# A fused attention and two-MLP block on one core: the mask stored once, block means in half the products, and a re-ordered front

## The chip, the cores and the metric

The kernel runs on one core of one Trainium2 chip. The metric is the device time of one execution in microseconds (us), the median of several runs; lower is better. The engines are PE (TensorE: matrix products, with its weight loads shown apart as PEld), DVE (VectorE), ACT (ScalarE), POOL (GpSimd) and SP (SyncE, which here issues all DMA transfers). Each engine works through its own list of instructions in order, and waits on semaphores for the others.

## The reference, cut to what matters

Two batches of 768 tokens, 8 heads of 64. An attention over near keys and block maxima feeds a token mixer, and that feeds a gated channel MLP.

```python
k_sum = k.reshape(B, H, 24, 32, D).max(axis=3)        # block maxima
v_sum = v.reshape(B, H, 24, 32, D).mean(axis=3)       # block means
scores_l = where(|i - j| < 16, scale * q @ k.T, -1e9) # near keys: the mask
scores_s = scale * q @ k_sum.T + log(32)              # far: 24 block maxima
a = softmax(concatenate([scores_l, scores_s]))
x = a @ concatenate([v, v_sum])                       # (2, 768, 512) after the heads are joined
h = relu(x.T @ w_tok1) @ w_tok2                       # token mixer
u = x + h.T
x2 = u + relu(u @ w_ch1) @ w_ch2                      # channel mixer
# then: token shift, k = relu(xk @ w_k), v = k*k @ w_v, r = sigmoid(xr @ w_r)
out = r * v
```

## The kernel before

The attention is worked in 12 *units* of 128 queries, 6 for each batch (units 0 to 5 and 6 to 11). For a unit, PE writes scores of 8 heads against the 64 near keys of each 32-query block and against the 24 block maxima (`sc`), and adds the mask by two more products (L304): the mask is split into an indicator of the query's place in its block (128 columns) and rows of 0 or -1e30 over 64 keys, four times side by side for the four head pairs, in three kinds (first unit, middle, last). Both stand in the 34 upper partitions of each half of the tile `msk`, so `load_mask` issues two loads of 34 partitions x 896 numbers. DVE takes maxima and subtracts them (`max`, L309 and L311), ACT takes the exponentials (`en`, `ef`), PE transposes them (`tr`, L337), ACT copies them out (`tc`, L341), and PE multiplies them with the values and the block means (`pv`, L348 and L355). DVE divides (`norm`), ACT and DVE split the result into a high and a low part (`xh`, `xl`), and PE multiplies these with the token weights (`t1`, three products of 128x512 at L191 to L193 for each half). After six units the hidden rows are split by `t1h` (ACT, L464) and `t1l` (DVE), and `t2` multiplies them with the second token weights on top of transposes of x (L497 and L505).

The block means come from `vs`: 13 steps a batch, each with 4 products of a 128x64 indicator with 65 columns of one head group of the values (L272). `vd` copies them to where `pv` reads them. `vu` (POOL) fills the overlapping value windows.

The weights arrive as pairs of 64-bit words and are turned into F32 by `ca` (ACT, L395), an optional `cn` (ACT, L402), and `cj` (DVE); `cj` needs one instruction more (L407) where `cn` was not run. Then `ch` (ACT, L412) and `cl` (DVE, L415) make the high and the low part.

Nothing schedules this at run time: a long string `PLAN` lists the steps with their arguments, and each step appends its instructions to the lists of its engines. So the order in `PLAN` is the order on each engine. Loads have no natural wait, so the plan paces them by *gates* (`gv`, `gq`, `gx`, `gk`, ...): a 4-byte DMA that reads a tile and so holds SP, and every transfer behind it, until that tile is written (`gx 2` waits for the normalised x of unit 2). PSUM has two single banks (`ps`: transposes, `t2`) and three pairs (`pp`: `sc`, `vs`, `pv`, `t1`), SBUF has 48 slots of 4 KB per partition, all handed out in turn.

Order of the first batch before: the scores of units 0 to 5 come early, four units of them ahead of the first transposes; the steps of `vs` are cut into the transposes of units 1 and 2 and then run in one stretch; `pv` and `t1` follow. All six token weights are loaded in one burst behind the values. Keys and values of the second batch are loaded behind `gx 2` and `gx 3`.

Of the kernel before, what the change touches and what calls it, by code (L numbers as in the profile page):

```python
# [44 lines left out]
PLAN = """heat 6,vz 0,vz 1,lk 0 0,lk 0 1,km 0 0,lq 0 0 0,lk 0 2,km 0 1,lk 0 3,lq 0 0 1,km 0 2,msk,lq 0 1,cst,km 0 3,sc 0,pad 0,max 0  # L45
gq 0 0,lq 0 2,lv 0,sc 1,en 0,gq 0 1,lv 1,lv 2,ef 0,pad 1,max 1,sc 2,en 1,ef 1,gq 0 2,lv 3,lv 4,pad 2,max 2,sc 3,tr 0 0,gv 0
lv 5,ld t1 0,gv 2,ld t1 1,gv 4,ld t1 2,en 2,tc 0 0,ef 2,pad 3,max 3,tr 0 1,sc 4,tc 0 1,en 3,vs 0 0,vs 0 1,ef 3,tr 1 0,pad 4
max 4,vs 0 2,vs 0 3,tc 1 0,pad 5,vu 0,vu 1,tr 1 1,sc 5,tc 1 1,en 4,vs 0 4,vs 0 5,tr 2 0,ef 4,max 5,vs 0 6,vs 0 7,ca t1 0
tc 2 0,vu 2,vu 3,vs 0 8,vs 0 9,tr 2 1,ca t1 1,vs 0 10,tc 2 1,vs 0 11,vs 0 12,cj t1 0,tr 3 0,tr 3 1,vd 0,vu 4,vu 5,gv 5
ld t2 0,tc 3 0,pv 0,cj t1 1,tc 3 1,ch t1 0,ld t2 1,ca t1 2,cl t1 0,pv 1,norm 0,xh 0,cj t1 2,en 5,tr 4 0,ef 5,ld t2 2,xl 0  # L50
pv 2,norm 1,tc 4 0,tr 4 1,xh 1,t1 0,xl 1,pv 3,ch t1 1,norm 2,tc 4 1,mu,cl t1 1,gx 1,xh 2,norm 3,tr 5 0,gx 2,lk 1 0,t1 1,xl 2
tc 5 0,tr 5 1,ch t1 2,pv 4,tc 5 1,xh 3,gx 3,lk 1 1,cl t1 2,xl 3,pv 5,t1 2,ca t2 0,lk 1 2,norm 4,cj t2 0,ca t2 1,xh 4,ca t2 2
norm 5,xl 4,gk 1 0,lk 1 3,ch t2 0,gk 1 1,lv 6,cl t2 0,t1 3,gk 1 2,lv 7,xh 5,cj t2 1,t1 4,gk 1 3,lv 8,xl 5,ch t2 1,cj t2 2
vs 1 0,vs 1 1,t1 5,gv 6,lv 9,cl t2 1,ch t2 2,vs 1 2,om,vs 1 3,t1h 0 0,cl t2 2,gv 7,vu 6,lv 10,t1h 0 1,vs 1 4,vs 1 5,t1l 0 0
t1l 0 1,gv 8,vu 7,lv 11,km 1 0,vs 1 6,t2 0 0 0,km 1 1,gv 9,vu 8,ld c 0 0,km 1 2,t2 0 1 0,t2h 0 0 0,km 1 3,gv 10,vu 9,ld c 1 0
t2l 0 0 0,vs 1 7,vs 1 8,t2h 0 1 0,vs 1 9,gv 11,vu 10,vu 11,lq 1 0,vs 1 10,vs 1 11,t2 0 2 0,ca c 0 0,t2l 0 1 0,cj c 0 0,lq 1 1
ca c 1 0,t2 0 3 0,ch c 0 0,cj c 1 0,gu 0 1 0,lq 1 2,t2h 0 2 0,t2l 0 2 0,ch c 1 0,vs 1 12,sc 6,t2h 0 3 0,cl c 0 0,vd 1
t2l 0 3 0,t2 0 0 1,pad 6,cl c 1 0,t2 0 1 1,max 6,t2h 0 0 1,sc 7,t2h 0 1 1,en 6,sc 8,pad 7,ef 6,max 7,tr 6 0,pad 8,tr 6 1,sc 9
tc 6 0,max 8,tc 6 1,en 7,t2 0 2 1,pad 9,ef 7,max 9,tr 7 0,t2h 0 2 1,sc 10,tc 7 0,en 8,tr 7 1,pv 6,pad 10,max 10,tc 7 1,en 9
ef 8,ef 9,tr 8 0,norm 6,tr 8 1,sc 11,tc 8 0,tc 8 1,en 10,tr 9 0,pad 11,max 11,ef 10,tr 9 1,pv 7,tc 9 0,tc 9 1,xh 6,t2 0 3 1  # L60
en 11,xl 6,ef 11,norm 7,c1 0 0,t2h 0 3 1,xh 7,xl 7,tr 10 0,c1h 0 0,pv 8,tc 10 0,c1l 0 0,tr 10 1,c1 0 1,norm 8,tc 10 1,xh 8
xl 8,tr 11 0,c1h 0 1,pv 9,tc 11 0,c1l 0 1,tr 11 1,pv 10,norm 9,tc 11 1,xh 9,pv 11,norm 10,xl 9,xh 10,t1 6,norm 11,gq 1 0
ld c 0 1,gq 1 1,ld c 2 0,gq 1 2,ld c 1 1,ld c 3 0,gu 0 3 1,ld c 2 1,ld c 3 1,gx 8,ld c 4 0,ld c 5 0,ld c 4 1,gx 9,ld c 6 0
gx 10,ld c 5 1,ca c 0 1,t1 7,xl 10,cn c 0 1,ld c 7 0,ca c 2 0,cj c 0 1,ca c 3 0,t1 8,ld c 6 1,ch c 0 1,cn c 2 0,cl c 0 1,t1 9
cn c 3 0,ld c 8 0,cj c 2 0,ca c 1 1,cj c 3 0,c2 0 0 0,ch c 2 0,ld c 9 0,c2 0 0 1,ch c 3 0,cl c 2 0,cn c 1 1,c2 0 0 2,cl c 3 0
ca c 2 1,c2 0 0 3,ld c 7 1,cj c 1 1,cn c 2 1,c1 0 2,ch c 1 1,cj c 2 1,ld c 8 1,ca c 4 0,cl c 1 1,ch c 2 1,ca c 5 0,cl c 2 1
ld c 10 0,t1 10,cn c 4 0,c1h 0 2,cj c 4 0,cn c 5 0,ld c 11 0,c2 0 1 0,c1l 0 2,ch c 4 0,c2 0 1 1,cj c 5 0,ca c 3 1,cl c 4 0
c2 0 1 2,ld c 9 1,ch c 5 0,c2 0 1 3,cn c 3 1,cl c 5 0,c1 0 3,xh 11,ld c 10 1,cj c 3 1,ca c 4 1,xl 11,ch c 3 1,ld c 11 1
cn c 4 1,cl c 3 1,ca c 6 0,cj c 4 1,c2 0 2 0,c1h 0 3,wst e 1 0,c2 0 2 1,ch c 4 1,c1l 0 3,c2 0 2 2,ca c 7 0,cl c 4 1,cn c 6 0
c2 0 2 3,wst e 1 1,cn c 7 0,c1 0 4,cj c 6 0,ca c 5 1,cj c 7 0,gx 11,ch c 6 0,ch c 7 0,cl c 6 0,cn c 5 1,cl c 7 0,c2 0 3 0  # L70
ca c 6 1,cj c 5 1,wst e 1 3,c2 0 3 1,c1h 0 4,ch c 5 1,c2 0 3 2,c1l 0 4,cn c 6 1,c2 0 3 3,cl c 5 1,ca c 8 0,cj c 6 1,c1 0 5
ca c 9 0,ch c 6 1,cn c 8 0,cl c 6 1,cn c 9 0,cj c 8 0,c2 0 4 0,ca c 7 1,cj c 9 0,c1h 0 5,c2 0 4 1,ch c 8 0,c1l 0 5,t1 11
ch c 9 0,cl c 8 0,cn c 7 1,cl c 9 0,wst e 2 0,c2 0 4 2,ca c 8 1,cj c 7 1,c2 0 4 3,t1h 1 0,t1h 1 1,c1 0 6,t1l 1 0,wst e 2 1
# [824 lines left out]
```

## Time and profile before

| | |
|---|---|
| runs | 466.26, 464.44, 466.57 us; median 466.26 |
| profiled execution | 465.3 us, span 463.0 us (first to last instruction) |
| granted TensorE clock | 0.999 |
| PE busy | 447.0 us (97%), 4420 matmuls |
| DVE, ACT, POOL busy | 364.2 us (79%), 277.1 us (60%), 40.2 us (9%) |
| DMA | 106.27 MB, 230 GB/s on average |

The page cuts the span into 40 slices and gives each engine's busy tenths:

```profile
PE   7789999999999998999999999999999999999996
PEld 3567787888888888989898998888989999999995
DVE  3757977476788438898968719989899979998955
ACT  1467357488996443386544338987987654763620
POOL 1680690000000000000000000000000000000000
```

A slice is 11.6 us. In the rows further down, a line of the timeline begins with its start and its length, then engine, source line, operation, output<-inputs and count; what stands in brackets is how long the engine had been idle before it and what ended that. "issue" there means that the engine waited for nothing that the profile shows. A product of F32 operands counts as two matmul records, a transpose as one. "PEclk" is the clock granted to PE as a share of its full 2.4 GHz. "DMA share" is the mean busy share of the 16 DMA engines.

### The profile page before, as it was taken

How to read it: one execution, taken by the hardware profiler on the slowest of the kernel's cores; microseconds unless marked ns; L12 is line 12 of the kernel's file. 1: busy time of each engine (PE TensorE's matmuls, PEld its weight loads, DVE VectorE, ACT ScalarE, POOL GpSimd, SP SyncE). 2: the span in 40 equal slices, each digit the busy share in tenths (PEclk: the TensorE clock that was granted, in tenths of full speed). 3: DMA queues.
4: the chain of work that ended last, by engine and by line, in shares of the span. 5: the costliest groups of instructions: out<-in, count | busy, mean ns of one | idle time of the engine just before them, and what ended most of it. 6: DMA issues, size and time to landing. Idle time of an engine off the chain costs nothing.

```text
span 463.0 us, 10930 instructions
## 1 busy us (share of the span) xinstructions
PE 447.0 (97%) x4420; PEld 392.4 (85%) x4420; DVE 364.2 (79%) x581; ACT 277.1 (60%) x499; POOL 40.2 (9%) x110
## 2 busy tenths in 40 slices
PE   7789999999999998999999999999999999999996
PEld 3567787888888888989898998888989999999995
DVE  3757977476788438898968719989899979998955
ACT  1467357488996443386544338987987654763620
POOL 1680690000000000000000000000000000000000
...
GB/s 251 257 222 128 216 184 48 293 316 403 95 127 189 174 45 1 259 286 2 209 380 275 303 392 214 336 390 91 376 340 361 292 361 191 315 296 133 341 0 91
DMA packets 34803, 106.27 MB, mean 230 GB/s; under 512 B 3710, under 2 KB 10306, under 8 KB 34754
## 3 DMA queue, kind: packets, MB, share of 16 engines
...
## 4 chain that ended last, share of the span: by engine, by line
PE 81%; DVE 4%; issue 1%; ACT 0%; DVEq 0%
PE p L191 8%; PE p L192 8%; PE p L193 8%; PE acc L191 7%; PE acc L193 7%; PE acc L192 7%; PE v L193 4%; PE v L191 4%; PE v L192 4%; PE r L191 2%; PE h L193 2%; PE r L192 2%; PE h L192 2%; PE r L193 2%; PE h L191 2%; PE u L505 2%
## 5 line engine op out<-in xcount | busy, mean ns | idle before, releaser
L700 DVE TENSOR_TENSOR ev<-p,ev 128x512 f32<-128x512 f32 x84 | 56.2, 686 | 21.0 <-PE p L193 17.8
L191 PE MATMUL p<-xs,wba 128*128 128x256 f32 x168 | 47.4, 282 | 1.6 <-DVE ev L700 1.6
L191 PE MATMUL v<-wbv,k 128*128 128x256 f32 x168 | 47.1, 280 | 0.0
L192 PE MATMUL v<-wbv,k 128*128 128x256 f32 x168 | 47.1, 280 | 0.0
L193 PE MATMUL v<-wbv,k 128*128 128x256 f32 x168 | 47.1, 280 | 0.0
L192 PE MATMUL p<-xs,wba 128*128 128x256 f32 x168 | 47.0, 280 | 0.0
L193 PE MATMUL p<-xs,wba 128*128 128x256 f32 x168 | 47.0, 280 | 0.0
L191 PE MATMUL acc<-hq,wc 128*128 128x512 f32 x96 | 37.8, 394 | 0.0
L193 PE MATMUL acc<-hq,wc 128*128 128x512 f32 x96 | 37.8, 393 | 0.0
L192 PE MATMUL acc<-hq,wc 128*128 128x512 f32 x96 | 37.7, 393 | 0.0
L191 PEld LDWEIGHTS p<-xs,wba 128*128 128x128 f32 x168 | 31.6, 188 | 2.1 <-DVE ev L700 2.0
L191 PEld LDWEIGHTS v<-wbv,k 128*128 128x128 f32 x168 | 31.8, 189 | 0.1
L192 PEld LDWEIGHTS v<-wbv,k 128*128 128x128 f32 x168 | 31.8, 189 | 0.1
L193 PEld LDWEIGHTS v<-wbv,k 128*128 128x128 f32 x168 | 31.8, 189 | 0.0
L192 PEld LDWEIGHTS p<-xs,wba 128*128 128x128 f32 x168 | 31.6, 188 | 0.1
L193 PEld LDWEIGHTS p<-xs,wba 128*128 128x128 f32 x168 | 31.6, 188 | 0.0
L570 ACT ACTIVATE hq<-ev 128x512 fp32r<-128x512 f32 x24 | 14.9, 632 | 24.2 <-DVE ev L700 24.2
L693 ACT COPY ev<-p 128x512 f32<-128x512 f32 x12 | 7.0, 587 | 36.3 <-PE p L193 36.3
L191 PE MATMUL p<-xs,wae 128*128 128x256 f32 x88 | 24.8, 282 | 1.2 <-ACT wae L446 1.2
L704 ACT ACTIVATE ev<-ev 128x512 f32<-128x512 f32 x24 | 15.1, 632 | 16.8 <-DVE ev L700 16.5
L192 PE MATMUL p<-xs,wae 128*128 128x256 f32 x88 | 24.8, 282 | 0.0
L193 PE MATMUL p<-xs,wae 128*128 128x256 f32 x88 | 24.7, 281 | 0.0
...
## 6 DMA issues: line engine op xcount, KB each, us to landing
...
```

The lines of the kernel that those rows point to most:

```text
L191: PE.matmul(o, lhsT=wh, rhs=xh, start=start, stop=False)
L192: PE.matmul(o, lhsT=wh, rhs=xl, start=False, stop=False)
L193: PE.matmul(o, lhsT=wl, rhs=xh, start=False, stop=stop)
L505: PE.matmul(ps[:, dst:dst + m], lhsT=h1[b, k][:, low, d], rhs=x[:, i, o:o + m], start=False, stop=low == 1 and k == 1 and pi == len(pieces ...
L570: A.activation(out=h2_block(c, d, q, 0), in_=x, func=AF.Relu)
L693: A.copy(out=block(z, c, d, 0), in_=pr[z, c, d, 0])
L700: V.tensor_tensor(out=block(z, c, d, o), in0=pr[z, c, d, p], in1=block(z, c, d, x), op=ALU.add)
L704: A.activation(out=x, in_=x, func=AF.Relu)
```

## The change

The diff touches four things.

1. The mask's 64 key columns are stored once for each kind of unit, and the product reads them four times by a step of 0 between the head pairs. The array in memory has 128 partitions, both halves filled (rows 34 to 63 of each half hold zeros), so one load of 128x320 numbers brings it. `PLAN` has it fourth among the loads, where it was seventh and eighth.
2. A step of `vs` makes 2 products of 130 columns in place of 4 of 65, from the same values into the same places.
3. `tok2` is split: the transposes of x can be issued alone (`t2x`), and `t2` issues them only if that has not been done. There is a new gate `gt` on the transposed exponentials of a unit.
4. The first 352 of the 1704 steps in `PLAN` are put in another order (362 steps now); from there on the lists agree. Eleven steps are new (`gv 1`, `gv 3`, `gt 3`, `gx 0`, `cn` for the token weights but the first, `t2x 0 0 0`, `t2x 0 1 0`), and `gv 4` is gone. Token weights now go out one by one: the first behind `gv 3`, the second behind `gv 5`, the third behind `gt 3`, the next three behind `gx 0`, `gx 1` and `gx 2`. The second batch's first keys wait for `gx 3`, and its remaining keys and values go out in turns, each behind a gate on a load two or three places earlier. `t1 6` and `t1 7` stand ahead of `pv 10` and `pv 11`.

```diff
-MW = NP * 64
-PLAN = """heat 6,vz 0,vz 1,lk 0 0,lk 0 1,km 0 0,lq 0 0 0,lk 0 2,km 0 1,lk 0 3,lq 0 0 1,km 0 2,msk,lq 0 1,cst,km 0 3,sc 0,pad 0,max 0
+PLAN = """heat 6,vz 0,vz 1,lk 0 0,lk 0 1,km 0 0,lq 0 0 0,msk,lk 0 2,km 0 1,lk 0 3,lq 0 0 1,km 0 2,lq 0 1,cst,km 0 3,sc 0,pad 0,max 0
...
     def load_mask():
-        for i in range(2):
-            load(msk[64 * i:64 * i + MR], mask)
+        load(msk, mask)
...
-    msk = c_p.tile([P, P + 3 * MW], BF16, name="msk")
+    msk = c_p.tile([P, P + 3 * 64], BF16, name="msk")
...
-        for p in range(NP):
-            r, g = 64 * (p % 2), p // 2
-            PE.matmul(vs[b][r:r + 64, 0, VW * g:VW * g + VW], lhsT=x, rhs=vw[QT * b + t][:, j, VW * p:VW * p + VW],
-                      start=(w == 0 and g == 0), stop=(w == 12 and g == 1), tile_position=(0, r))
+        v = vw[QT * b + t][:, j, :].rearrange("k (g h d) -> k g h d", g=2, h=2)
+        for h in range(2):
+            o = vs[b][64 * h:64 * h + 64, 0, 0:2 * VW].rearrange("n (g d) -> n g d", g=2)
+            PE.matmul(o, lhsT=x, rhs=v[:, :, h, :], start=(w == 0), stop=(w == 12), tile_position=(0, 64 * h))
...
+    def each_pair(m):
+        return bass.AP(m.tensor, m.offset, [list(m.ap[0]), [0, NP], [1, 64]])
...
-        r = P + MW * (0 if t == 0 else 2 if t == QT - 1 else 1)
+        r = P + 64 * (0 if t == 0 else 2 if t == QT - 1 else 1)
...
-            PE.matmul(near, lhsT=msk[d, 0:P], rhs=msk[d, r:r + MW].rearrange("k (p n) -> k p n", p=NP), start=False, stop=True, tile_position=(64 * i, 0))
+            PE.matmul(near, lhsT=msk[d, 0:P], rhs=each_pair(msk[d, r:r + 64]), start=False, stop=True, tile_position=(64 * i, 0))
...
-    def tok2(b, dt, g):
+    def tok2_x(b, dt, g):
...
+    def tok2(b, dt, g):
+        if (b, dt, g) not in ups:
+            tok2_x(b, dt, g)
...
+"gt": lambda u: gate(et[u][:, 0, 0:1])
```

Three places show how the lists move. The first is SP's list at the very start: the loads of the first batch (`kp` keys, `q` queries, `msk` mask, `cst` constants with the identity, `vw` values, `gate_sb` a gate). Before:

```order
L196 DMA kp_0_96<-in_kT 128x800
L196 DMA kp_1_99<-in_kT 128x800
L196 DMA q_0_103<-in_qT 128x512
L196 DMA kp_2_105<-in_kT 128x800
L196 DMA kp_3_109<-in_kT 128x800
L196 DMA q_0_103<-in_qT 128x512
L196 DMA msk<-in_mask 34x896 x2
L196 DMA q_1_116<-in_qT 128x1024
L196 DMA cst<-in_const 128x280
L196 DMA gate_sb<-q_0_103 1x1
L196 DMA q_2_162<-in_qT 128x1024
L196 DMA vw_164<-in_vp 128x2x260
```

And now:

```order
L195 DMA kp_0_96<-in_kT 128x800
L195 DMA kp_1_99<-in_kT 128x800
L195 DMA q_0_103<-in_qT 128x512
L195 DMA msk<-in_mask 128x320
L195 DMA kp_2_106<-in_kT 128x800
L195 DMA kp_3_110<-in_kT 128x800
L195 DMA q_0_103<-in_qT 128x512
L195 DMA q_1_115<-in_qT 128x1024
L195 DMA cst<-in_const 128x280
L195 DMA gate_sb<-q_0_103 1x1
L195 DMA vw_161<-in_vp 128x2x260
L195 DMA gate_sb<-q_1_115 1x1
```

The mask is one transfer ahead of the third and fourth key tile, and the values `vw` of unit 0 stand ahead of the third query tile and the gate on the second query tile.

The second is PE's list between two units' scores: `vs` are the block means, `et` transposes of the exponentials `e`, `sc` the scores. Before, between the scores of units 4 and 5:

```order
L272 MATMUL vs_364<-vw_164,cst 64x65 x8
L337 MATMUL et_375<-cst,e_208 128x128 x4
L272 MATMUL vs_364<-vw_203,cst 64x65 x8
L337 MATMUL et_409<-cst,e_208 128x128 x2
L298 MATMUL sc_412<-kp_0_96,q_2_162 32x128 x8
```

And now, between the scores of units 2 and 3:

```order
L338 MATMUL et_247<-cst,e_154 128x128 x4
L338 MATMUL et_257<-cst,e_154 128x128 x2
L271 MATMUL vs_269<-vw_161,cst 64x130 x4
L271 MATMUL vs_269<-vw_200,cst 64x130 x4
L299 MATMUL sc_280<-kp_0_96,q_1_115 32x128 x8
```

The six transposes of a unit stand together, the means have half as many products of twice the columns, and this pattern repeats between all later scores; before, four units of scores stood ahead of it.

The third is ACT's list around the end of the first token product: `wt` are the high parts of token weights, `rawt` their raw words, `h` the hidden rows of `t1h`, `uc` the result of `t2`. Before:

```order
L412 CAST wt_1_915<-rawt_1_586 128x512
L412 CAST wt_2_938<-rawt_2_643 128x512
L464 ACTIVATE h_00_949<-t_692 128x512
L464 ACTIVATE h_01_961<-t_692 128x512
L526 CAST uc_0_1033<-u_0_0_988 128x512
L526 CAST uc_1_1054<-u_1_0_1016 128x512
```

And now:

```order
L396 ACTIVATE rawt_2_795<-rawt_2_795 128x512
L403 ACTIVATE rawt_2_795<-rawt_2_795 128x512
L413 CAST wt_1_882<-rawt_1_693 128x512
L465 ACTIVATE h_00_893<-t_685 128x512
L465 ACTIVATE h_01_895<-t_685 128x512
L413 CAST wt_2_931<-rawt_2_795 128x512
L533 CAST uc_0_994<-u_0_0_921 128x512
```

The last two conversions are split up: the raw words of the last weight are worked on right ahead of the hidden rows, with one instruction more (`cn`), and its high part `wt_2` is now made behind both hidden rows.

## Rows read from the trace of the kernel before

**Rows 1.** Windows: stretch, length, busy us (xinstructions) per engine, PEclk, DMA share, GB/s

```profile
10.50:33.00 22.50, 17.44 (x534) 13.15 (x536) 13.89 (x18) 11.71 (x26) 16.32 (x33) 1.00 0.77 251
33.00:54.00 21.00, 20.09 (x465) 15.78 (x466) 17.87 (x34) 12.09 (x22) 5.08 (x13) 1.00 0.50 146
54.00:70.00 16.00, 15.72 (x328) 13.98 (x328) 13.29 (x19) 7.35 (x16) 14.76 (x34) 1.00 0.60 192
70.00:180.00 110.00, 109.92 (x1114) 90.39 (x1112) 75.10 (x120) 75.43 (x142) 0.58 (x4) 1.00 0.50 178
```

**Rows 2.** Timeline of PE, first scores: start, us, operation, count, idle before

```profile
10.04 0.45 PE L298 MATMUL sc<-kp,q 64*32 64x128 f32 x16 [0.52 <-issue]
10.85 0.28 PE L304 MATMUL sc<-msk 34*128 34x256 bf16 x1 [0.36 <-DMA msk<-in_mask]
12.10 0.28 PE L304 MATMUL sc<-msk 34*128 34x256 bf16 x1 [0.96 <-DMA msk<-in_mask]
12.31 1.16 PE L298 MATMUL sc<-kp,q 64*32 64x128 f32 x64
...
13.61 1.16 PE L298 MATMUL sc<-kp,q 64*32 64x128 f32 x64
...
16.33 1.07 PE L298 MATMUL sc<-kp,q 64*32 64x128 f32 x54 [0.98 <-issue]
```

**Rows 3.** Windows without engines: length, PEclk, DMA share, GB/s around 10.5 us

```profile
9.00:10.50 1.50, 1.00 0.90 330
10.50:12.10 1.60, 1.00 0.49 155
```

**Rows 4.** Windows of PE alone, cut where PE stood still

```profile
0.00:16.32 16.32, 11.91 (x220) 1.00 0.75 247
16.33:20.98 4.65, 3.39 (x127) 1.00 0.97 263
20.99:26.58 5.59, 5.23 (x127) 1.00 0.93 315
26.59:32.58 5.99, 4.89 (x126) 1.00 0.61 235
32.58:36.60 4.02, 4.01 (x158) 1.00 0.01 4
```

**Rows 5.** Timeline of PE, 21 to 35 us

```profile
21.21 0.69 PE L272 MATMUL vs<-vw,cst 128*64 128x65 f32 x16
21.82 0.66 PE L337 MATMUL et<-cst,e 128*128 128x128 f32 x4
...
32.84 0.72 PE L348 MATMUL xo<-vbd,et 64*128 64x130 f32 x8
33.49 0.86 PE L355 MATMUL xo<-vw,et 64*32 64x65 f32 x64
34.28 0.66 PE L337 MATMUL et<-cst,e 128*128 128x128 f32 x4
```

**Rows 6.** Timeline of PE, means of the second batch

```profile
49.53 0.69 PE L272 MATMUL vs<-vw,cst 128*64 128x65 f32 x16 [0.34 <-DMA vw<-in_vp]
...
53.47 0.45 PE L272 MATMUL vs<-vw,cst 128*64 128x65 f32 x8 [0.57 <-DMA vw<-in_vp]
...
57.71 1.39 PE L272 MATMUL vs<-vw,cst 128*64 128x65 f32 x40
```

**Rows 7.** Timeline of SP, two places: start, us of issue, DMA

```profile
13.27 0.59 SPq L196 DMA_DIRECT2D gate_sb<-q  x1
...
39.33 0.38 SPq L196 DMA_DIRECT2D kp<-in_kT  x1
```

**Rows 8.** Lines by form of ACT to 200 us: busy, mean ns | idle

```profile
L402 ACT ACTIVATE rawc<-rawc 128x512 uint32<-128x512 uint8 x22 | 14.4, 675 | 0.0
...
L412 ACT CAST wt<-rawt 128x512 fp32r<-128x512 f32 x6 | 4.0, 670 | 3.0 <-DVE rawt L408 3.0
...
L464 ACT ACTIVATE h<-t 128x512 fp32r<-128x512 f32 x4 | 2.2, 595 | 0.4 <-PE t L193 0.4
```

More of the change, by code (lines that the diff above doesn't have):

```diff
@@ L49 @@
[L49 to L53, printed above, removed]
@@ new lines @@
+t2x 0 0 0,t2x 0 1 0,ch t2 2,vs 1 2,om,vs 1 3,cl t2 2,vu 6,t1l 0 0,t1l 0 1,vu 7,km 1 0,t2 0 0 0,vs 1 4,vs 1 5,km 1 1,gv 9,vu 8
+ld c 0 0,t2 0 1 0,vs 1 6,t2h 0 0 0,gv 10,vu 9,ld c 1 0,t2l 0 0 0,km 1 2,vs 1 7,vs 1 8,t2h 0 1 0,vs 1 9,gv 11,vu 10,vu 11
+lq 1 0,vs 1 10,vs 1 11,t2 0 2 0,ca c 0 0,t2l 0 1 0,km 1 3,cj c 0 0,lq 1 1,ca c 1 0,t2 0 3 0,ch c 0 0,cj c 1 0,gu 0 1 0,lq 1 2
+t2h 0 2 0,t2l 0 2 0,ch c 1 0,vs 1 12,sc 6,t2h 0 3 0,cl c 0 0,vd 1,t2l 0 3 0,t2 0 0 1,pad 6,cl c 1 0,t2 0 1 1,max 6,t2h 0 0 1
@@ new lines @@
+c2 0 6 2,cl c 9 1,cn c 11 1,c2 0 6 3,cl c 10 1,wh e 2 5,t2 1 2 0,wh e 2 6,cj c 11 1,wh e 2 4,wl e 2 5,c1 0 8,t2h 1 2 0
+wl e 2 6,wst e 2 5,ch c 11 1,ws e 2 3,cl c 11 1,wh e 2 2,ld e 1 2,wl e 2 4,t2 1 3 0,c1h 0 8,wl e 2 2,ld e 1 3,c1l 0 8
+c2 0 7 0,t2h 1 3 0,c2 0 7 1,bs 0 1 0,bs 0 1 2,c2 0 7 2,ld e 1 0,bs 0 1 1,c2 0 7 3,t2 1 0 1,bs 0 1 3,bh 0 1 0,wst e 2 6
+bl 0 1 0,ca e 1 2,c1 0 9,bh 0 1 1,wst e 2 4,t2h 1 0 1,bl 0 1 1,cn e 1 2,wst e 2 2,ca e 1 3,cj e 1 2,cn e 1 3,t2 1 1 1
+ca e 1 0,cj e 1 3,cn e 1 0,ws e 1 0,c2 0 8 0,cj e 1 0,t2h 1 1 1,c2 0 8 1,ws e 1 1,c2 0 8 2,ws e 1 2,c2 0 8 3,t2 1 2 1,c1h 0 9
@@ new lines @@
+c2 1 9 2,wh e 0 0,cj e 0 2,c2 1 9 3,ca e 0 3,wst a 0 0,wl e 0 0,c2 1 10 0,cn e 0 3,c2 1 10 1,ca e 0 1,cj e 0 3,c2 1 10 2
+cn e 0 1,ws e 0 0,c2 1 10 3,ca a 0 1,cj e 0 1,c2 1 11 0,cn a 0 1,ws e 0 1,c2 1 11 1,wh e 0 1,ws e 0 2,c2 1 11 2,wh e 0 5
+wl e 0 1,wh e 0 6,c2 1 11 3,wl e 0 5,ca a 0 2,p 0 1 0 0,ld a 0 3,wl e 0 6,wh e 0 4,ws e 0 3,cn a 0 2,p 0 1 0 1,wl e 0 4
+pc 0 1 0,cj a 0 1,wh e 0 2,cj a 0 2,p 0 1 0 5,wh e 0 3,pa 0 1 0 0,wl e 0 2,gh 1 0 0,p 0 1 0 6,pa 0 1 0 1,gl 1 0 0,p 0 1 0 4
+ca a 0 3,pa 0 1 0 2,cn a 0 3,wl e 0 3,wh a 0 1,p 0 1 0 2,pa 0 1 0 3,pa 0 1 0 4,p 0 1 0 3,cj a 0 3,bh 0 2 0,pa 0 1 0 5
```

185 lines of the change are left out of this document (89 added, 96 removed).

## The prediction

> **What bounds the kernel now.** I first read the windows by stage. From 70 us on PE is busy without a gap (109.92 of 110 us to 180 us), so PE's own work sets the end there and the change leaves that work almost as it is [rows 1]. Before 70 us PE stands still for 22.50 - 17.44 = 5.06 us up to 33 us, 0.91 us up to 54 us and 0.28 us up to 70 us. Those 6.25 us, and PE work that goes, are what the change can win; time won before 70 us reaches the end if the loads behind it also move.
>
> Then I read PE's timeline. The scores of the first unit are through at 10.04 + 0.45 = 10.49 us, but its two mask products wait for their loads, and unit 1 starts at 12.31 us [rows 2]. In the same stretch the 16 DMA engines fall from 0.90 to 0.49 busy [rows 3], while the gate on the second query tile holds SP until 13.27 us [rows 7]: a few engines still work while most have run dry. The two mask loads of 34 partitions are the odd ones in that list, so I take them for the cause.
>
> The third view is PE alone, cut where it stops and the profile names no releaser. The stops come after 220 matmuls and then after 127, 127 and 126 [rows 4]. A fixed number of instructions and no data behind it: these are fetches of PE's own instructions. Three blocks took 4.66, 5.60 and 6.00 us from one resumption to the next while the DMA engines were 0.97, 0.93 and 0.61 busy; with DMA at 0.01, 158 matmuls pass in 4.02 us without a stop. So until 33 us PE is bound by how fast blocks of about 128 matmuls arrive, and that depends on what else is in the DMA queues. The stops cost 0.98 us [rows 2] and 1.26 + 0.36 + 1.10 us, 3.7 us with 0.15 of another wait in it.
>
> The Trainium skill, "Runtime: NRT & Kernel Launch", section "Instruction fetch mechanics", says that instructions come in blocks of 256, that the next block is fetched while the current one runs, and that crossing a block is mostly hidden. The trace agrees on the size (127 matmuls with their weight loads are 254 instructions) and not on the hiding. By that rule the stops would be something else and an even spread would not shrink them: the sum below would be 463.2; it is the first rival.
>
> **The change part by part.**
>
> *Mask.* One load of 80 KB over all partitions now stands ahead of two key tiles. At 330 GB/s [rows 3] it delays them by 0.25 us; two mask products add 0.2 us each. Unit 1 then starts at 10.49 + 0.25 + 0.4 = 11.15 us and not at 12.31: -1.15 us. Unit 2 needs the second query tile; it follows only if that lands by 12.45 us, where the gate now passes at 13.27. If that tile stays late, 0.4 us are left; the most is the whole wait, 0.36 + 0.96 = 1.3 us. I take -1.15, since the engines that were dry from 10.5 us had time to bring it. The step of 0 over the pairs changes no column count: 0.
>
> *Order and fetches.* The block after matmul 220 came 3.8 us after PE entered the block before it (220 - 128 = 92; 12 matmuls for warming up and 66 for unit 0 come first, so this is inside unit 1's scores, about 12.55 us; resumed at 16.33). That entry moves to 11.4 us, so the block comes at 15.2 us. PE now has units 1 and 2 (2.6 us, at 1.3 us a unit by the starts at 12.31 and 13.61 [rows 2]), six transposes (0.9 us, from four in 0.66 [rows 5]) and the first means: it is there at 14.8 us and stops for 0.4. The next 128 matmuls are one unit and a third of scores, six transposes and seven steps of means, 1.75 + 0.9 + 1.7 = 4.3 us, against a fetch between 4.66 and 5.60 us, since the values and the third query tile are in the queues as before: 0.8 us of stop at 5.1. The third block holds scores, transposes and means in the same mix, 4.1 us, with fewer weights under way: 4.5 us, a stop of 0.4. After that products with the values come in (72 matmuls in 34.28 - 32.84 = 1.44 us [rows 5]) mixed with transposes, 4 us a block, and I expect none. Left: 1.6 us of 3.55: -2.0 us. Bounds: 0 if each fetch just takes longer, -3.55 if all go.
>
> *Means.* A step has 4 matmul records of 130 columns in place of 8 of 65. The old ones took 0.61 us for 16 (21.21 to 21.82), 38 ns each [rows 5], and at most 1.39 us for 40 in a long run, 35 ns [rows 6]: 0.28 us a step. A record of 130 columns is in the trace only with wider weights: 0.65 us for 8, 81 ns (32.84 to 33.49) [rows 5]. If the new record costs 35 ns, 26 steps save 3.6 us; at 81 ns they cost 0.32 us each and 1.1 us more. Half the weight load of the 81 ns row and its columns: I take 60 ns, 0.24 us a step, -1.0 us.
>
> *Loads of the second batch.* PE waits 0.34 and 0.57 us for values there [rows 6]. Their chain starts with the keys, issued at 39.33 us [rows 7], behind `gx 2` before and `gx 3` now. PE comes some 4 us earlier to this place, but the gate is one unit later in the plan (about 3 us of products), so the chain starts only some 2 us earlier; the means, on the other hand, are now spread over the second token products and need the last values later. I take half of the waits as gone, -0.5 us; bounds -0.9, and +1.5 if the last values are late by that.
>
> *First second-token product.* It needs the low part of the last token weight. Its high part now stands on ACT behind both hidden rows, and those wait for the last `t1`: 2 x 0.595 + 0.67 [rows 8], and about 0.65 for the low part on DVE, 2.5 us. PE's cover is four steps of means (0.96 us) and the eight transposes issued ahead (0.9 us): +0.6 us; without the transposes 1.5, and 0 if ACT reaches it in time.
>
> *The rest.* Five `cn` cost ACT 5 x 0.675 = 3.4 us [rows 8] between 25 and 47 us and take an instruction each off DVE; from 33 to 54 us ACT was busy for 12.09 of 21 us, DVE for 17.87 [rows 1], so this is the right way round: 0, and up to +1 if ACT, which works in order, holds back a high part that PE needs. The early transposes and `t1 6`, `t1 7` only change places in a stretch where PE is full: 0.
>
> Sum: -1.15 - 2.0 - 1.0 - 0.5 + 0.6 = -4.05. The profiled execution took 465.3 us, 1 us under the median of 466.26: from it the sum gives 461.25, from the median 462.2. I forecast 461.6.
>
> **The rivals.** *The stops stay.* If the fetch time grows as PE waits less, or the stops are not fetches, 2.0 us come back: 463.2 from the profiled time. For it: the same values and queries move in the same 12 to 20 us. Against it: their length followed the DMA share.
>
> *Won and given back.* PE arrives 4 us earlier at 70 us, and the channel weights set the pace from 80 us on. For it: nothing in the windows shows how close those loads are. Against it: they are gated on slots that the attention of the second batch frees, so they move along, and PE has 0.08 us of idle time there [rows 1]. Then 465.
>
> *Slower: one late gate.* Every transfer of the second batch stands on SP behind `gx 3`, that is behind the normalised unit 3; on DVE this stands behind the joining of the third token weight, which is loaded only behind the new `gt 3`. I have that load landing near 31 us and unit 3's products done near 36, 5 us of slack. If it lands 10 us late, the keys go out at 43.6 us in place of 39.33, PE waits 4.3 us more than now for scores and means, the means' -1.0 and the mask stay inside that wait, and the time is about 469. It decides from about 36 us on. Against it: nothing else is in the queue then (DMA 0.01 from 32.58 us before [rows 4]).
>
> **How the numbers follow.** Forecast 0.60, its own range 459 to 463.8; the stops stay 0.20; given back 0.13; slower 0.07. Linear bounds of the terms reach from about 456 to 470, never all at once; leaving out a tenth on each side gives 458.3 to 465.6. A difference of 0.5%, 2.3 us, is about what a measurement of this kernel can tell from none: faster means under 463.9, slower over 468.6. Nearly all of the forecast and over half of the first rival are faster (0.58 + 0.11), the rest of them and the second rival the same: 0.69, 0.24, 0.07.
>
> **What would show it.** The profile after should have unit 1's scores starting near 11.2 us and the gate on the second query tile before 12.5; stops of PE again every 126 to 128 matmuls, but of some 1.6 us in sum; 4 records a step of means at 50 to 70 ns; the last `t1` and the first `t2` some 4 us earlier; and from 70 to 180 us no more idle time than now. Wrong would be a PE that stands as long before 33 us as now, means at 81 ns, or a wait for `vw`, `kp` or `wt` above 1.5 us between 45 and 65 us.

## The result, and the profile after

| | before | after |
|---|---|---|
| median of 9 runs each (us) | 464.97 (464.10 to 467.45) | 467.85 (467.05 to 468.46) |
| ratio of the times | | 1.0052, interval 1.0033 to 1.0071 |
| profiled execution, its span (us) | 465.3, 463.0 | 467.86, 466.1 |
| granted clock | 0.999 | 0.996 |
| PE busy (us), matmuls | 447.0, 4420 | 449.5, 4316 |

The change is slower by 0.5%; I had forecast 461.6 us, faster than before, with a range up to 465.6. The first view is again the windows by stage, now of the changed kernel (columns as in [rows 1]; 65 to 70 us stands there a second time by itself):

```profile
10.50:33.00 22.50, 18.54 (x569) 14.11 (x562) 13.69 (x18) 12.67 (x30) 15.74 (x35) 1.00 0.60 172
33.00:54.00 21.00, 20.53 (x372) 15.24 (x372) 16.36 (x31) 13.88 (x25) 6.16 (x15) 1.00 0.71 210
54.00:70.00 16.00, 13.06 (x186) 11.37 (x188) 10.56 (x15) 6.00 (x15) 13.74 (x32) 0.89 0.67 208
65.00:70.00 5.00, 5.00 (x106) 4.46 (x108) 4.24 (x6) 2.81 (x10) 3.32 (x12) 0.66 0.26 104
70.00:180.00 110.00, 110.00 (x1211) 88.72 (x1195) 72.98 (x115) 73.83 (x140) 0.20 (x2) 1.00 0.51 178
```

Up to 33 us PE stands still for 3.96 us in place of 5.06, up to 54 us for 0.47 in place of 0.91: so far the change wins. From 54 to 70 us it stands for 2.94 us in place of 0.28, and from 65 to 70 us the granted clock is 0.66, which means that PE ran at the lower of its two levels (1.2 GHz) for much of it. Behind 70 us PE is full, as before. What was lost was lost in one place. PE's timeline shows it (start, length, operation, count, idle before):

```profile
10.54 0.28 PE L305 MATMUL sc<-msk 34*128 34x256 bf16 x2
10.76 1.16 PE L299 MATMUL sc<-kp,q 64*32 64x128 f32 x64
...
12.06 1.16 PE L299 MATMUL sc<-kp,q 64*32 64x128 f32 x64
...
14.76 1.27 PE L271 MATMUL vs<-vw,cst 128*64 128x130 f32 x16 [0.49 <-DMA vw<-in_vp]
15.97 1.25 PE L299 MATMUL sc<-kp,q 64*32 64x128 f32 x64
...
20.09 1.39 PE L271 MATMUL vs<-vw,cst 128*64 128x130 f32 x16 [1.85 <-DMA vw<-in_vp]
...
25.11 0.45 PE L271 MATMUL vs<-vw,cst 128*64 128x130 f32 x4 [0.48 <-DMA vw<-in_vp]
...
28.75 1.00 PE L349 MATMUL xo<-vbd,et 64*128 64x130 f32 x8 [1.09 <-ACT vbd L277]
...
57.89 0.67 PE L271 MATMUL vs<-vw,cst 128*64 128x130 f32 x8 [0.85 <-DMA vw<-in_vp]
...
64.87 1.15 PE L299 MATMUL sc<-kp,q 64*32 64x128 f32 x64 [2.09 <-DMA q<-in_qT]
```

The first four lines are the mask as forecast: its two products (10.54) wait for nothing, unit 1 starts at 10.76 (12.31 in [rows 2]) and unit 2 follows at 12.06. Then come waits for the values at 14.76, 20.09 and 25.11 and one for `vbd` at 28.75, 3.91 us together. From 10.5 to 33 us no stop is left for which the profile names no releaser; [rows 2, 4] have four. At 57.89 PE waits for values again, and at 64.87 unit 6 starts after 2.09 us of waiting for its query tile. In the kernel before, the same line of PE reads:

```profile
63.57 1.15 PE L298 MATMUL sc<-kp,q 64*32 64x128 f32 x64 [0.23 <-DMA q<-in_qT]
```

Only 0.23 us of wait, but also there unit 6 starts right when the tile has come. The queue of SP tells why the tile is not earlier although PE was. After (start, us of issue, transfer):

```profile
11.08 0.60 SPq L195 DMA_DIRECT2D gate_sb<-q  x1
...
40.06 0.58 SPq L195 DMA_DIRECT2D gate_sb<-xf  x1
40.69 0.88 SPq L195 DMA_DIRECT2D kp<-in_kT  x2
43.92 0.58 SPq L195 DMA_DIRECT2D gate_sb<-kp  x1
...
58.88 0.81 SPq L195 DMA_DIRECT2D q<-in_qT  x2
...
64.80 0.59 SPq L195 DMA_DIRECT2D gate_sb<-q  x1
```

The gate on the second query tile passes at 11.08 (13.27 in [rows 7]). The keys of the second batch go out at 40.69, behind the gate on unit 3 that passed at 40.06; before, they went out at 39.33 [rows 7], behind unit 2. Before, the same gate on unit 3 and the query tile stood here:

```profile
40.89 0.58 SPq L196 DMA_DIRECT2D gate_sb<-xf  x1
...
57.48 1.10 SPq L196 DMA_DIRECT2D q<-in_qT  x2
```

So unit 3 was normalised only 0.83 us earlier than before (40.06 against 40.89), not 4 us, and the key load that hangs on it now comes 1.36 us later than the one that hung on unit 2. From there to the query tile it is a chain of loads and gates, each held until the one ahead has landed: 18.2 us before, 18.2 us after. That the two are equal is chance: in the profiles below the same stretch takes 13.7 to 21.5 us. The marks in one table (us; product starts and issues from the timelines of PE and SP, the end is the span):

| | before | after | difference |
|---|---|---|---|
| scores of unit 1 | 12.31 | 10.76 | -1.55 |
| end of the last `t1` of the first batch | 51.82 | 49.20 | -2.62 |
| first keys of the second batch issued | 39.33 | 40.69 | +1.36 |
| first query tile of the second batch issued | 57.48 | 58.88 | +1.40 |
| scores of unit 6 | 63.57 | 64.87 | +1.30 |
| first channel product (`c1 0 0`) | 81.81 | 84.68 | +2.87 |
| end | 463.0 | 466.1 | +3.1 |

In these two executions PE won 2.6 us and gave it all back in front of unit 6, with 1.3 us on top. Another 1.6 us are lost between unit 6 and the first channel product, where the clock was low, and 0.2 us behind that.

**The theories tested.** A: unit 6 starts when its query tile lands, at the end of the chain that begins with the second batch's first keys; the wait in front of it also costs the clock. B: PE's own work, its instruction fetches or the channel weights behind set the time, so that an earlier chain changes nothing.

### The profile page after: what moved, and what is told of

The parts are those of the page before. It is cut to its first block, busy times and chain, and to the rows that moved or that the text cites. A ratio compares the mean times of both kernels' runs of the same rounds, so it can differ in the third digit from the quotient of the medians.

```text
span 466.1 us, 10720 instructions
## 1 busy us (share of the span) xinstructions
PE 449.5 (96%) x4316; PEld 391.9 (84%) x4316; DVE 361.1 (77%) x576; ACT 279.2 (60%) x504; POOL 39.6 (8%) x110
## 4 chain that ended last, share of the span: by engine, by line
PE 81%; DVE 7%; DMA 5%; ACT 2%; SPq 2%; issue 1%; DVEq 0%; ACTq 0%
PE p L190 8%; PE p L191 8%; PE p L192 7%; PE acc L192 7%; PE acc L190 7%; PE acc L191 7%; PE v L192 4%; PE v L190 4%; PE v L191 4%; PE u L512 3%; DMA q<-in_qT 3%; PE r L190 2%; PE h L192 2%; PE r L192 2%; PE h L191 2%; PE r L191 2%
```

## The experiments

All ratios are to the kernel before, run beside each of them on the same chip. This table has the marks of the profiled executions (us) for all kernels; the sections follow.

| kernel | keys issued | query tile issued | unit 6 | end | ratio (interval) |
|---|---|---|---|---|---|
| before | 39.33 | 57.48 | 63.57 | 463.0 | 1 |
| after | 40.69 | 58.88 | 64.87 | 466.1 | 1.0052 (1.0033 to 1.0071) |
| e1, mask alone | 36.72 | 56.15 | 63.01 | 462.5 | 0.9961 (0.9935 to 0.9988) |
| e2, means alone | 38.02 | 56.89 | 63.38 | 468.7 | 1.0069 (1.0032 to 1.0106) |
| e3, order alone | 42.19 | 59.70 | 65.93 | 466.1 | 1.0089 (1.0058 to 1.0119) |
| e12, after with old means | 40.10 | 57.41 | 63.46 | 465.0 | 1.0034 (1.0010 to 1.0058) |
| e4, after, query ahead | 39.50 | 55.95 | 62.22 | 463.5 | 1.0033 (1.0008 to 1.0059) |
| e5, after, products in the wait | 40.24 | 58.09 | 64.19 | 464.2 | 1.0012 (0.9996 to 1.0027) |
| e6, after, keys behind unit 2 | 36.53 | 58.03 | 63.90 | 463.6 | 0.9980 (0.9952 to 1.0008) |
| e7, after, old gates first | 38.83 | 57.96 | 64.06 | 464.6 | 1.0064 (1.0040 to 1.0088) |
| e9, after with e4, e6, e7 | 35.78 | 53.41 | 60.55 | 462.1 | 1.0019 (0.9986 to 1.0052) |
| e10, after with e4, e6 | 38.67 | 56.30 | 63.90 | 464.0 | 0.9992 (0.9967 to 1.0017) |
| e14, e9, conversions later | 37.80 | 55.90 | 62.50 | 465.0 | 0.9985 (0.9951 to 1.0020) |
| e11, before, keys behind unit 3 | 42.02 | 59.18 | 65.29 | 465.1 | 1.0032 (1.0014 to 1.0051) |
| e15, e2 with `t1 6` earlier | 38.42 | 56.38 | 64.42 | 464.3 | 1.0021 (0.9990 to 1.0052) |
| e8, e1, query ahead | 38.38 | 54.37 | 62.53 | 462.1 | 0.9956 (0.9934 to 0.9978) |
| e13, e8, conversions later | 39.35 | 53.09 | 62.01 | 461.3 | 0.9947 (0.9927 to 0.9966) |

The marks are of one execution each, the ratios of medians, and a mark alone decides little. Kernels whose lists agree up to the second batch's keys issue them at different times: e1, e8 and e13 at 36.72, 38.38 and 39.35 us, e6 and e10 at 36.53 and 38.67, the change, e5 and e4 at 40.69, 40.24 and 39.50. The profiled executions of e3, e4, e7 and e9 are the fastest of theirs. In 16 of the 17 profiles the end comes 399.3 to 402.5 us after unit 6 starts (405.3 in e2), but that spread of 3.2 us is as large as the whole loss, and some medians do not follow unit 6: e4 and e12 start it no later than the kernel before and are slower by 0.3%, e9 starts it 3 us earlier and is no faster.

Of theory A's forecasts, those for e3, e5, e6 and e11 came true in the ratio against B's. Those for e7 and e9 failed and e10's came halfway; e4 and e8 came out at B's number (e8's interval just reaches A's).

### The three parts, each alone

The mask alone (e1), the means alone (e2), and the order with old mask and old means (e3):

```diff
-            load(msk[64 * i:64 * i + MR], mask)      # e1: twice, 34 partitions
+        load(msk, mask)                              # once, 128 partitions
-        for p in range(NP): PE.matmul(...65 columns) # e2: 4 products a step
+        for h in range(2):  PE.matmul(...130 columns)# 2 products a step
-PLAN of before                                       # e3
+PLAN of after
```

> The kernel before with the mask part of the change alone (one load of 128 x 320, read by a step of 0; its place in the order of loads is that of before). Both theories look at where the front's microseconds end. Theory A (chain of loads: the second batch's first scores start when the first query tile of that batch has landed, at the end of a chain of gated loads that begins with the gates gx on the normalised units 2 and 3; what PE wins elsewhere is waited off there): unit 1 starts 1.2 to 1.5 us earlier, gx 2 about 1 us earlier, so the query tile lands about 1 us earlier and the time falls by 0.5 to 1.3 us. Theory B (PE's own work sets the time, what changed is what PE's instructions cost): the 1.3 us of waiting for the mask go, -1.3 us, wherever the loads are.

> The kernel before with the block means alone changed (2 products of 130 columns a step in place of 4 of 65). The trace of the changed kernel shows 16 records in 1.21 us (14.76 to 15.97), 76 ns each, 0.30 us a step where the old form took 0.28. Theory A (chain of loads): almost nothing, -0.3 to +0.3 us, since PE waits in front of the second batch's scores anyway. Theory B (PE's own work): 26 steps of 0.02 us more, +0.5 us; my prediction had -1.0 us.

> The changed kernel with the old mask loads and the old means: the new order alone. Theory A (chain of loads): the new order delays the chain (keys of the second batch at 40.69 us in place of 39.33), so this kernel carries the loss by itself: +2.5 to +4 us against the kernel before, slower than the changed kernel by up to 1 us because the mask's tail is back. Theory B (PE's own work): without the new means the loss is smaller, +1 to +2 us.

Measured: the mask wins 0.39% (1.8 us, more than the 1.3 of waits; the mean granted clock of its ten executions was 0.999, against 0.995 before, and what that is worth is not shown), the order loses 0.89% (4.1 us, as A forecast), the means lose 0.69% (3.2 us, which neither theory had). The parts do not add up: their sum would be about +5.5 us, the change lost 2.4. The order alone has the chain's mark: keys at 42.19, unit 6 at 65.93 after 2.4 us of waiting for the query tile; part of the 42.19 is its front, where the first scores waited 1.60 us for the maxima of a key tile at 11.71. The mask alone has the keys at 36.72 in this profile, but at 38.38 and 39.35 in e8 and e13. In e2 the end comes 405.3 us after unit 6, and PE's timeline has a hole that no other kernel has:

```profile
92.17 0.86 PE L355 MATMUL xo<-vw,et 64*32 64x65 f32 x64
92.97 0.72 PE L348 MATMUL xo<-vbd,et 64*128 64x130 f32 x8
93.61 0.86 PE L355 MATMUL xo<-vw,et 64*32 64x65 f32 x64
98.25 0.77 PE L191 MATMUL t<-xhl,wt 128*128 128x512 f32 x1 [3.78 <-DVE wc L415]
```

The line at 98.25 names DVE, but one thing speaks against a wait for data: the product that stands there is matmul number 2000, and the stops of the kernel before came after 220 and then every 127 [rows 4]; 220 + 14 x 127 = 1998. The block before it had been passed in 2.0 us (64 + 8 records in 1.44 us). So I took it for a fetch of instructions, and found the fetch in the view of the DMA queues, which gives packets, MB and share of the 16 engines; queue q8 is PE's instructions. The first row is of e2, 95.8 to 96.9 us, the second of the kernel before, 13.9 to 15.0 us:

```profile
q8 instruction: 1, 0.02, 5.6%
```

```profile
q8 instruction: 1, 0.02, 5.4%
```

One packet of 16 KB in each. The packets of the kernel before start at 13.94, 18.66, 24.32 and 30.14 us, its PE resumes at 16.33, 21.00, 26.60 and 32.59 [rows 4]: 2.3 to 2.5 us later each time. In e2 the packet starts at 95.84 and PE resumes at 98.25: 2.4 us.

The stop cost more than its 3.78 us, for the granted clock was low behind it (from 98.20 to 104 us; the kernel before passes 27 records in that stretch):

```profile
98.20:104.00 5.80, 5.75 (x14) 0.53 0.99 374
```

Nor is it in every execution, it seems: three of the ten took 465.2 to 465.8 us, the others 469.1 to 471.6.

The Trainium skill, "Runtime: NRT & Kernel Launch", section "Instruction fetch mechanics", calls the crossing of a block mostly hidden. Between 70 and 180 us the profiles of before and after agree, with no stop at any end of a block; the 3.78 us of e2 and the stops of [rows 4] do not.

### The stop tried: one product moved (e15)

e2 with unit 6's first token product ahead of unit 10's products with the values, as the change's order has it:

```diff
-pv 10,norm 9,tc 11 1,xh 9,pv 11,norm 10,xl 9,xh 10,t1 6
+t1 6,pv 10,norm 9,tc 11 1,xh 9,pv 11,norm 10,xl 9,xh 10
```

> The kernel before with the new means and one move of the change's order: unit 6's first token product ahead of unit 10's products with the values. Theory (the 3.78 us in which PE stands ahead of that product with the means alone are an instruction fetch: the block before passes in 2.0 us, a fetch takes about 6): the block now takes 4.8 us, the stop is below 1.3 us, ratio 1.000 to 1.002. Rival (that product waits for DVE's conversions of channel weights): it waits as long in its new place, 3 us or more, ratio 1.006 or more.

Measured: ratio 1.0021. PE's timeline there:

```profile
96.02 0.81 PE L355 MATMUL xo<-vw,et 64*32 64x65 f32 x58
97.41 0.31 PE L355 MATMUL xo<-vw,et 64*32 64x65 f32 x6 [0.57 <-issue]
97.65 0.50 PE L191 MATMUL t<-xhl,wt 128*128 128x512 f32 x1
```

`t1 6` no longer waits, and 0.57 us of stop stand in the middle of the 64 records of one `pv`, after 58 of them, where no semaphore is waited for: it is again at matmul 2000. That settles the place: the hole belongs to a count of instructions, not to an operation. With 104 matmuls fewer the ends of the blocks fall elsewhere, and the means alone put one behind a block that passes faster than the next can be fetched. The change's own profile has no such stop; it mixes `t1 6` and `t1 7` with the `pv`. That the stop makes up the 3.2 us of the medians is likely, not shown: the intervals of e2 and e15 overlap.

In place, the new means cost little: e12 is the change with the old ones.

```diff
-        for h in range(2): ... v[:, :, h, :]                   # 130 columns
+        for p in range(NP): ... vw[...][:, j, VW * p:VW * p + VW] # 65 columns, as before
```

> The changed kernel with the means as in the kernel before (8 records of 65 columns a step). Theory A (the new means cost no more than 0.3 us in themselves, the loss is the chain's): ratio near 1.005, as the change. Rival C (the 3.2 us that the means cost alone are the products' own): ratio near 0.998. By the fetch of instructions the means alone cost a stop that depends on where blocks of 127 products end, so this kernel, with other ends, need not show it.

1.0034 against 1.0052 with the new means: 0.8 us of difference, and the intervals overlap. In its profile unit 6 starts at 63.46, as before, after 1.97 us of waiting for the query tile. The end is 2.0 us later all the same, and behind the wait the clock was low:

```profile
65.00:70.00 5.00, 5.00 (x116) 0.75 0.02 6
```

### The chain, shortened and lengthened (e6, e4, e10, e11)

e6 issues the first two keys behind unit 2, e4 the query tiles ahead of two channel weights of 512 KB (whose conversions move behind the first half of the second token products), e10 both. e11 does the reverse of e6 to the kernel before.

```diff
 e6:  gx 2,ld t2 2
+lk 1 0,lk 1 1
 ... gx 3
-lk 1 0,lk 1 1
 e4: -gv 9,vu 8,ld c 0 0 ... gv 10,vu 9,ld c 1 0 ... lq 1 0 ... lq 1 1
     +gv 9,vu 8,lq 1 0 ... gv 10,vu 9,lq 1 1 ... ld c 0 0 ... ld c 1 0
 e11: -gx 2,lk 1 0 ... gx 3,lk 1 1
      +gx 2 ... gx 3,lk 1 0,lk 1 1
```

> The changed kernel with the first two key loads of the second batch issued behind the gate on unit 2 in place of unit 3; the gates on keys and values behind them stay. Theory A (the chain of gated loads sets unit 6): keys go out near 37.6 us in place of 40.69, the query tile lands near 62, PE's wait of 2.09 us for it goes and the clock stays up: ratio near 0.997. Rival B (PE's own work or the channel weights set it): the keys come earlier and the end moves by less than 0.5 us, ratio near 1.005.

> The changed kernel with two pairs of loads exchanged: the first two query tiles of the second batch ahead of the first two channel weights (512 KB each), and the conversion of these weights moved behind the last second-token results, since ACT and DVE work in order. Theory A (chain of loads): the query tile is issued near 56.3 us in place of 58.88, lands near 61 to 62 in place of 64.8, PE's wait of 2.09 us before unit 6 goes to under 0.3 us, the clock does not fall, and the time is 2.5 to 3.5 us below the changed kernel, about that of the kernel before. Theory B (PE's own work): the wait in front of unit 6 moves to another place, 0 to -0.5 us.

> The changed kernel with the second batch's first two keys behind the gate on unit 2 and its first query tiles ahead of the first two channel weights; the first batch's loads stay as changed. Theory A: the query tile is issued near 55 us, unit 6 starts near 61.8, ratio near 0.996. Rival B: no more than the query tiles ahead gave alone, 1.003.

> The kernel before with one edit of the change's order: its first key load of the second batch behind the gate on unit 3 in place of unit 2. Theory A (the chain sets unit 6 in the kernel before as well): keys near 41.5 us in place of 39.33, the query tile 1 to 1.5 us later, PE waits for it by that more (0.23 before), and the time rises by 1.2 to 3 us: ratio 1.003 to 1.007. Rival B (PE's own work sets unit 6 there): ratio 1.000.

e11 is the plain test, on a kernel that has nothing of the change but this one load's place. SP now (keys, then query tile, then the gate that waits for it):

```profile
42.02 1.64 SPq L196 DMA_DIRECT2D kp<-in_kT  x3
...
59.18 0.81 SPq L196 DMA_DIRECT2D q<-in_qT  x2
...
65.01 0.59 SPq L196 DMA_DIRECT2D gate_sb<-q  x1
```

Keys 2.7 us later, query tile 1.7 later, unit 6 at 65.29, 1.7 later, end 2.1 later, ratio 1.0032 with 1 outside its interval. Theory B had forecast 1.000; it falls. But PE does not wait for the query tile here, as A had it. It waits for the values of the same chain, 1.46 and 0.77 us where [rows 6] have 0.34 and 0.57; another 0.7 us it was late before (its clock was 0.83 from 10 to 20 us, 1.00 in the profile of the kernel before):

```profile
51.33 0.69 PE L272 MATMUL vs<-vw,cst 128*64 128x65 f32 x16 [1.46 <-DMA vw<-in_vp]
...
55.47 0.45 PE L272 MATMUL vs<-vw,cst 128*64 128x65 f32 x8 [0.77 <-DMA vw<-in_vp]
```

e10 gains 0.6% on the change, clear of the intervals, and e4 0.2%, within them; both have no wait for the query tile left. For e4 theory A had forecast 2.5 to 3.5 us, and it won 0.8. In its profile unit 6 starts at 62.22, earlier than before, but PE then stands for 0.78 us without a releaser and for 0.80 us for the exponentials of unit 6, and the first channel product comes at 82.24 (81.81 before).

e6 came out at the forecast ratio (0.998, forecast 0.997), but not in the forecast way:

```profile
36.53 1.77 SPq L195 DMA_DIRECT2D kp<-in_kT  x2
...
43.18 0.55 SPq L195 DMA_DIRECT2D gate_sb<-kp  x1
...
58.03 0.81 SPq L195 DMA_DIRECT2D q<-in_qT  x2
```

The keys went out 4.2 us earlier and passed their gate only 0.7 us earlier (43.18 against 43.92); a token weight of 512 KB was issued 0.4 us ahead of them, which I take for the reason. The query tile came 0.85 us earlier, and PE still waited 2.12 us for it. Unit 6 starts 0.97 us earlier than in the change and the end comes 2.5 us earlier; most of the rest is the clock, which stayed up behind the same wait:

```profile
60.00:65.00 5.00, 2.88 (x82) 1.00 0.99 376
65.00:70.00 5.00, 5.00 (x155) 1.00 0.08 28
```

### The clock behind the wait (e5)

Nine bf16 products of 512 columns, used nowhere, between the last step of means and unit 6:

```diff
-ch c 1 0,vs 1 12,sc 6
+ch c 1 0,vs 1 12,wf 9,sc 6     # wf: PE.matmul(vs[1][:, 1, :], lhsT=warm[:, 0:P], rhs=warm)
```

> The changed kernel with nine more bf16 products of 512 columns (their result is used nowhere) between the last step of means and unit 6's scores, where PE waits 2.09 us for the query tile. Theory A (the clock): the 1.7 us that PE loses at the lower clock right behind that wait go, the granted clock stays 1.00 from 60 to 75 us, the first channel product starts near 83.0 us (84.68 without), ratio to before near 1.0015. Rival B (the channel weights behind set the time): the clock stays up as well, but PE then waits for weights between 85 and 110 us and the ratio stays near 1.005.

```profile
61.96 2.12 PE L262 MATMUL vs<-warm 128*128 128x512 bf16 x9
64.19 1.15 PE L303 MATMUL sc<-kp,q 64*32 64x128 f32 x64
```

```profile
65.00:70.00 5.00, 4.83 (x168) 1.00 0.10 39
```

The filler covers 2.12 us of the wait, the clock from 65 to 70 us is 1.00 (0.66 without), and from unit 6 to the first channel product it takes 18.64 us in place of 19.81. Ratio 1.0012, forecast 1.0015. So of the 1.8 us that the profile of the change loses behind unit 6, 1.2 us go with the lower clock; the rest I have not traced. (Unit 6 itself starts 0.68 us earlier than in the change, at 64.19, though nothing ahead of the filler differs: chance.) It is not the whole account: one of the nine executions of the change had a mean clock of 1.00 and took 468.01 us. And the profile of the kernel before, with a clock of 0.999, is not its usual execution: 108 executions beside the experiments have 0.995 on average, as the nine of the change have. So the medians of the two kernels do not differ by how much the clock is low, at most by where: in the profiles of e2, e3, e8, e11 and e15 it is 0.66 to 0.83 between 10 and 20 us.

### The first batch's gates (e7), and all together (e9, e14)

e7 gives the change the old order and gates of the first batch's loads; e9 adds e4 and e6; e14 moves the conversions of the first two channel weights behind the maxima of units 9 to 11.

```diff
 e7: -lv 0 ... gq 0 1,lv 1,lq 0 2 ... gv 0,lv 2 ... gv 1,lv 3 ... gq 0 2,lv 4,gv 2,lv 5 ... gv 3,ld t1 0 ... gv 5,ld t1 1
     +lq 0 2 ... lv 0,gq 0 1,lv 1 ... lv 2 ... gq 0 2,lv 3 ... lv 4,gv 0,lv 5,ld t1 0 ... gv 2,ld t1 1 ... gv 4
 e14: ca c 0 0 behind ef 6, ca c 1 0 behind tc 6 1, cj behind max 9 and max 10, ch behind en 9 and ef 9, cl behind norm 6 and max 11
```

> The changed kernel with the loads of the first batch's values, third query tile and first two token weights in the order and behind the gates of the kernel before. Theory A (the gates): the three waits for values before 26 us, 2.8 us in sum, fall below 1 us, units 0 to 3 are done about 2 us sooner, so the second batch's keys too (near 38.7 us in place of 40.69), ratio near 1.001. Rival B (transfers and instruction fetches share the queues): the value waits are replaced by stops of PE without a releaser every 127 matmuls, 2 to 3.5 us in sum, and the ratio stays near 1.005.

> The changed kernel with three edits together: the first batch's loads in the order and behind the gates of the kernel before, the second batch's first two keys behind the gate on unit 2, and its first query tiles ahead of the first two channel weights. Theory A (unit 6 starts when the query tile at the end of the chain of gated loads lands): the tile is issued near 54 us in place of 58.88, unit 6 starts near 61.5 in place of 64.87 without a wait for it, ratio to before near 0.994. Rival B (what PE wins is given back behind, whatever the chain does): unit 6 starts earlier, but the first channel sum is not earlier than 101 us and the ratio is 1.002 or more.

> The changed kernel with the four edits together: old order of the first batch's loads, keys behind the gate on unit 2, query tiles ahead of the channel weights, and the conversions of those weights behind the maxima of units 9 to 11. If the win of unit 6 (60.55 us) is given back to the conversions on DVE, the wait of 1.95 us for the exponentials falls below 0.8 us and the ratio is 0.997 to 0.999. Rival: the wait moves to the first channel product, ratio 1.002.

e7 was no better than the change (1.0064 for a forecast of 1.001; its profiled execution, 466.41 us, was the fastest of five). The value waits ahead of 26 us shrank from 2.8 us to one of 1.84, keys went out at 38.83, the query tile at 57.96, and PE waited 1.06 us for values and 2.26 for the tile: in this execution a win ahead of the chain is waited off at its end. The stops that rival B expected instead did not come (0.44 us in sum), so why the median is so high is open. In the profile of e9 the chain is short, unit 6 starts at 60.55, 3 us earlier than before, as forecast; then the next link holds PE:

```profile
60.55 1.16 PE L299 MATMUL sc<-kp,q 64*32 64x128 f32 x64
...
68.49 0.76 PE L338 MATMUL et<-cst,e 128*128 128x128 f32 x5 [1.95 <-ACT e L325]
```

1.95 us for the exponentials of unit 6, behind a DVE that is busy for 4.67 of the 5 us from 65 to 70. The median missed the forecast (1.0019 for 0.994) and came out at rival B's number (1.002 or more), that the win is given back behind. That profile is the fastest of its ten executions, 463.9 to 470.24 us; what spreads them I could not settle, since only one is profiled. In e14 that wait is 0.3 us at most, though its profile loses 2.93 us on the first values at 17.31; ratio 0.9985, with a spread of 461.8 to 468.4 us.

### The better kernel (e8, e13)

The kernel before with the new mask and e4's query tiles ahead (e8), and with the conversions moved as in e14 (e13).

```diff
 e8, on e1: -ld c 0 0 ... ld c 1 0 ... lq 1 0 ... lq 1 1
            +lq 1 0 ... lq 1 1 ... ld c 0 0 ... ld c 1 0
 e13, on e8: -t2l 0 3 0,ca c 0 0,ca c 1 0,cj c 0 0,ch c 0 0,cj c 1 0,ch c 1 0
             +ef 6,ca c 0 0 ... tc 6 1,ca c 1 0 ... max 9,cj c 0 0 ... max 10,cj c 1 0 ... en 9,ch c 0 0 ... ef 9,ch c 1 0
```

> The kernel before with the new mask and with the first query tiles of the second batch loaded ahead of the first two channel weights (their conversions moved behind the first token products). Theory A: the 1.2 us that PE waited for the query tile with the mask alone go, ratio near 0.9935 (462.0 us). Rival B (a later load sets the end): same as the mask alone, 0.9961.

> The kernel before with the new mask, the second batch's first query tiles ahead of the first two channel weights, and those weights' conversions moved behind the maxima of units 9 to 11. If the 0.62 us that PE waits for unit 6's exponentials in the run without the last move come from the conversions in front of them on ACT and DVE, the wait goes and the ratio is near 0.994. Rival: DVE is full from 65 to 75 us either way, PE waits as long for the exponentials or for the first channel product's weights, ratio 0.9956 as without the move.

463.79 and 463.09 us. e8's ratio is the one that rival B had forecast, that of the mask alone. In e13 unit 6 starts at 62.01 without a wait.

0.9947 (0.9927 to 0.9966) beats both kernels; the mask is most of it (0.9961 alone), and the steps from e1 to e8 to e13 are each within the intervals.

## Why the prediction was wrong, point by point

- **Mask, -1.15.** Right in its mechanism: -1.55 us at unit 1, unit 2 follows, and 1.8 us at the end when alone.
- **Order and fetches, -2.0.** This step failed. The stops were fetches, as read, and they went. But I took the values to be "in the queues as before". The new order puts each value load behind a gate, and the 3.7 us of stops became 3.9 us of waits for gated values and for `vbd`. The latter is ACT, which works in order:

```profile
26.97 0.70 ACT L396 ACTIVATE rawt<-rawt 128x512 f32<-128x512 f32 x1 [1.67 <-DMA rawt<-in_w]
27.57 0.44 ACT L328 ACTIVATE e<-e,logb 128x192 f32<-128x192 f32 x1
27.92 1.07 ACT L277 COPY vbd<-vs 32x130 f32<-32x130 f32 x4
```

  ACT's conversion of the first token weight waits 1.67 us for its load, `ef 4` and the copy to `vbd` stand behind it. I had bounded an in-order ACT at +1, but looked for it at the high parts, not here.
- **Means, -1.0.** Mis-sized: 16 records took 1.21 us (14.76 to 15.97), 76 ns each, twice a record of 65 columns. A step costs 0.30 us in place of 0.28, +0.5 in all. I had halved between the weight load of the 81 ns row and its columns; the new record, with other weights, costs nearly as much as that row. The other price, where fetches fall, I had not seen at all.
- **Loads of the second batch, -0.5.** The step that decided the sign. It said that "the chain starts only some 2 us earlier"; it started 1.36 us later, because unit 3 was done 0.83 us earlier and not 4; in none of the six profiles with the new order and the keys behind unit 3 (38.83 to 42.19) did it start 2 us earlier. And I sized it by the waits for values [rows 6]. The row that mattered was the 0.23 us of PE's wait for the query tile, which I did not read: a wait of almost nothing, but one that ends exactly with a landing, is a chain without slack. Its delay of 1.30 us went through whole, and 1.2 us of clock came with it, which no term had. In the ratios, that one load's place is worth 0.32% in the kernel before (e11), and putting it and its neighbour behind unit 2 in the change wins 0.7% (e6).
- **First second-token product, +0.6.** Mis-sized, 0.24 us.
- **The rest, 0.** `t1 6` and `t1 7` changing places was worth nothing to see, but with the new means the place of `t1 6` decides between a stop of 3.78 us (e2) and one of 0.57 (e15).
- **The rivals.** "Slower: one late gate", 0.07, had the place right: SP's chain behind `gx 3`. Its price and its point were wrong: I let it decide only where a late token weight pushed the keys to 43.6 us, and 40.69 without it went with the loss. "Won and given back" put the giving back at the channel weights behind 80 us; it was at 64.87. Of what would show me wrong I named waits for `vw`, `kp` and `wt`, and not the tile that was waited for.
